# One low part per block moved from GpSimd to VectorE, and a new order of sums for the last 256 tokens, in an attention and feed-forward kernel

## The chip, the cores and the metric

The kernel runs on one core of a Trainium2 chip. The metric is the device time of one execution in microseconds (us). Before the change it is 1053.36 us, the median of three runs (1052.81 to 1054.94). One more execution was taken by the hardware profiler: it took 1052.79 us, of which the span from the first to the last instruction is 1050.6 us.

In this text PE is TensorE's matmul row, DVE is VectorE, ACT is ScalarE, POOL is GpSimd and SP is SyncE. SP, ACT and POOL can issue DMAs.

## What is computed

```python
# q, k, v: (8, 8, 576, 64); w_in: (512, 2048); w_out: (2048, 512); alpha: (2048,)
scores = q @ k.T / 8, masked to key blocks (of 64) up to the query's own
attn = softmax(scores)
x = (attn @ v) as (4608 tokens, 512)
h = x @ w_in
g = max(h, 0) + alpha * min(h, 0)
out = g @ w_out
```

All inputs and outputs are float32.

## The kernel before

The kernel has two stages. Until about 590 us it does the attention, and beside it the feed-forward products for 6 of the 16 blocks of 128 hidden features (FA = 6); their part of the output goes to a DRAM tensor `part`. From then on it does the other ten feature blocks in five pairs (NG = 5), and this is the stage that the change touches. Tokens go in nine blocks of 512 (`t0`, CHB), each in two halves of 256 (`h`, CHA).

A product of two float32 matrices is made of reduced-precision ones: each operand is split into a high part (a cast, on ACT) and a low part (source minus high part, on DVE or POOL; `split`, L422 to L426), and three matmuls are summed: high by high, and the two mixed ones. On top of that, a pair of feature blocks is multiplied in the seven-product (Strassen-Winograd) form, which trades the eighth product for sums of operands and of results. In the first layer (`pair1`, L612) each of the seven products has 6 matmuls of 256 columns into a PSUM bank; DVE and ACT combine the seven and apply the activation (L635, L639, L539, L541) into a tile `R` for each half. For the second layer `parts_of` (L668) makes the operands from `R`: `ha`, the high and low part of three quarters of `R`, and `hs`, the high and low part of four sums of quarters `S` (four additions of 128 columns on POOL, L441; a cast of 512 columns on ACT, L424; and the low part of 512 columns, L425, on POOL by `SLO`). `pair2` (L687) then runs 21 matmuls: the products 0, 1 and 6 read `ha`, the products 2 to 5 read `hs`. They add up over the five pairs (`i` = 0 to 4) in four banks: product n lies in bank n // 2, half n % 2. In each group of three matmuls the first two read the high part and the third reads the low part. After the fifth pair `finish` (L705) combines the seven sums on ACT and DVE (L718, L715), adds `part` (L441) and stores to `out`. Where `(h, i)` = (0, 4), then, is the last pair of the first half of a block.

In the last 256 tokens (the second half of the last block; the argument `end` or `tail`) other lists of engines hold (TSADD, TALO, TSLO), the four result tiles are stored by themselves, and the last pair runs in the order of products (0, 1), (2, 3), (4, 5), (6).

The order of instructions on each engine isn't written out: a planner (`Plan.schedule`, L141) simulates the engines with costs that stand in the code, and each engine then takes, of the operations that are ready in this simulation, the one with the lowest `prio`. PE's priorities follow the order of the calls. The result is a fixed sequence for each engine, and an engine that comes to an instruction whose input is late waits there, with all that is behind it. On the chip only true data dependencies make anyone wait. The costs in the code that matter here, in ns, are

```python
LAT = {"PE": 240, "DVE": 140, "ACT": 137, "POOL": 95}   # from an end to a reader on another engine
LONGER, TO_POOL, BESIDE = 1.06, 85, 480
c_dve(n) = 65 + n / 0.96; c_pool(n) = 145 + 2.1 * n     # times LONGER
# low part: POOL c_pool(n) + 60; DVE c_dve(n), and up to BESIDE more while POOL is busy
```

The next block's first-layer pairs are called early (TURNS, L50): the seven products of its first pair stand behind the second-layer products of (0, 4) in the priorities. PSUM has eight banks; four of them hold the sums of `pair2`.

Of the kernel before, what the change touches and what calls it, by code (L numbers as in the profile page):

```python
# [22 lines left out]
P = 128  # L23
# [27 lines left out]
XWHEN, UW, UX0 = 1, -30, -20  # L51
AGAIN, UA, UL = ((1, 4), (0, 4)), -20, -6
# [266 lines left out]
def attn_ffn(ctx, tc, qT, kT, vT, w_in, w_out, alpha, out):  # L319
# [348 lines left out]
    def parts_of(R, i, tail):  # L668
# [18 lines left out]
    def pair2(i, parts, accs, end):  # L687
# [4 lines left out]
        def run(todo):  # L692
            for n, b, x, w in todo:
                for k, (u, v) in enumerate(((0, 0), (0, 1), (1, 0))):
                    nc.tensor.matmul(accs[n // 2]()[:, CHA * (n % 2):CHA * (n % 2) + CHA], b()[:, u, P * x:P * x + P], W()[:, v, 256 * W2AT[w]:256 * W2AT[w] + 256],  # L695
                                     start=(first and k == 0 and n % 2 == 0), stop=(last and k == 2 and (n % 2 == 1 or n == 6)))
        ha, hs = parts
        last3 = ((0, ha, 0, "11"), (1, ha, 2, "21")), ((2, hs, 1, "t2"), (3, hs, 2, "t3")), ((4, hs, 0, "t1"), (5, hs, 3, "22")), ((6, ha, 1, "t4"),)
        for todo in last3 if end else ((*last3[0], *last3[3]), (*last3[1], *last3[2])):
            b = todo[0][1]  # L700
            fseq[0] += len(todo) / 2
            op("PE", 3 * len(todo) * c_mm(CHA), lambda todo=todo: run(todo), claim=[W],
               r=[(b, "h"), (b, "l"), *[((W, W2AT[w] // 2 * 2), x) for *_, w in todo for x in "hl"]], w=[accs[n] for n in sorted({n // 2 for n, *_ in todo})], prio=1.0e6 + fseq[0])

    def finish(accs, t0, end):  # L705
# [5 lines left out]
        def m(n):  # L711
            return lambda: accs[n // 2]()[:, CHA * (n % 2):CHA * (n % 2) + CHA]

        def plus(to, n, u):
            op("DVE", c_dve(CHA), lambda: nc.vector.tensor_tensor(out=to(), in0=m(n)(), in1=u(), op=ALU.add), r=[accs[n // 2], u], w=[to], prio=due(UM))  # L715
            return to
        u1 = Buf("u")
        op("ACT", c_act(CHA), lambda: nc.scalar.copy(out=u1(), in_=m(0)()), r=[accs[0]], w=[u1], prio=due(UM))  # L718
        u2 = plus(Buf("u"), 2, u1)
# [309 lines left out]
```

## Time and profile before

| what | value |
|---|---|
| median of three runs | 1053.36 us |
| profiled execution, whole time | 1052.79 us |
| its span | 1050.6 us |
| PE busy in the span | 981.7 us, 93% |
| POOL busy in the span | 774.2 us, 74% |
| DVE busy in the span | 865.7 us, 82% |
| granted TensorE clock, mean | 0.97 of full speed |

The page cuts the span in 40 slices of 26 us and gives each engine's busy share in tenths. A timeline row has the start (us), the length (us), the engine, the line, the operation, the tiles and the count of instructions merged; in brackets stands how long the engine was idle just before, and who ended that. Buffer numbers are left out of the tiles' names: `t` is any tile of 512 float32 columns, `u` one of 256, `X` the operands of the first layer (and of the second in the last 256 tokens).

### The profile page before, as it was taken

What the parts mean: (1) busy time and instruction counts of PE and PEld (TensorE: products, weight loads), DVE (VectorE), ACT (ScalarE), POOL (GpSimd) and SP (SyncE); (2) the same over time, 40 slices, a digit from 0 to 9 for tenths busy, and PEclk for the clock granted to TensorE, in tenths of its full rate; (3) what the DMA queues carried; (4) which work ended last, traced back from release to release, by engine and by line L of the source; (5) the groups of instructions that cost most, each with busy time, mean ns of one, the idle gap of its engine ahead of it and who ended that gap; (6) DMA issues with size and microseconds to landing.
All of it is one profiled execution on the core that took longest, in us unless ns stands there. A gap on an engine that the chain in (4) does not pass through costs nothing. (4 is left out here: it accounts for less than half of the span.)

```text
span 1050.6 us, 35000 instructions
## 1 busy us (share of the span) xinstructions
PE 981.7 (93%) x13670; PEld 900.5 (86%) x13670; DVE 865.7 (82%) x1923; ACT 626.6 (60%) x2158; POOL 774.2 (74%) x1320
## 2 busy tenths in 40 slices
PE   4578999999999999999999999999999999999997
PEld 3356778889888888888888989999999999999997
DVE  6999899988888877866586987888888888888877
ACT  7878787877777676756564554535353535444442
POOL 5887567656566665656499898888887979797964
PEclk7679999999999999999999999999999999999999
DMA  8455767576576566442372602030303031221211
GB/s 314 155 191 182 232 201 239 167 246 205 180 220 218 187 193 209 145 153 91 106 260 92 248 21 91 32 100 22 101 22 100 22 101 42 80 56 67 62 41 61
DMA packets 86485, 143.30 MB, mean 136 GB/s; under 512 B 12336, under 2 KB 50224, under 8 KB 86320
## 3 DMA queue, kind: packets, MB, share of 16 engines
q1 hardware_dynamic: 85744, 140.67, 41.1%
q8 instruction: 107, 1.75, 0.7%
q14 instruction: 58, 0.48, 0.1%
q10 hardware_dynamic: 576, 0.40, 0.1%
HBM read 103.82 MB, written 37.22 MB: 134 GB/s over the span
## 5 line engine op out<-in xcount | busy, mean ns | idle before, releaser
L844 ACT ACTIVATE p<-duo,c 128x256 f32<-128x256 f32 (+8 forms) x576 | 221.5, 415 | 40.9 <-DVE c L839 28.7
L626 PE MATMUL bank<-X,w 128*128 128x256 f32 x1890 | 239.1, 284 | 4.2 <-DVE t L541 3.0
L626 PEld LDWEIGHTS bank<-X,w 128*128 128x128 f32 x1890 | 231.5, 191 | 6.4 <-DVE t L541 4.2
L808 POOL TENSOR_SCALAR c<-c 32x4 f32<-32x4 f32 (+3 forms) x400 | 100.6, 252 | 87.4 <-DVE c L836 59.8
L441 POOL TENSOR_TENSOR t<-t 128x128 f32<-128x128 f32 (+1 forms) x180 | 102.5, 579 | 58.4 <-DVE t L541 38.6
L695 PE MATMUL bank<-w,hs 128*128 128x256 f32 x1020 | 137.3, 284 | 5.8 <-POOL hs L425 5.8
L568 PE MATMUL bank<-wa,gh 128*128 128x512 f32 x432 | 137.7, 400 | 4.3 <-POOL gh L550 2.3
L695 PEld LDWEIGHTS bank<-w,hs 128*128 128x128 f32 x1020 | 128.4, 190 | 7.7 <-POOL hs L425 7.4
L844 ACT ACTIVATION_READ_ACCUMULATOR p<-duo,c 128x1 f32 x576 | 130.2, 227 | 0.0
L529 PE MATMUL bank<-xh,wa 128*128 128x256 f32 x864 | 125.8, 287 | 1.5 <-DVE g L541 1.3
L441 POOL TENSOR_TENSOR t<-t,t 128x128 f32<-128x128 f32 (+1 forms) x200 | 123.2, 622 | 3.8 <-DVE w L425 1.3
L836 DVE TENSOR_REDUCE c<-duo 128x2 f32<-128x512 f32 (+8 forms) x288 | 121.4, 476 | 5.5 <-PE duo L831 5.3
L529 PEld LDWEIGHTS bank<-xh,wa 128*128 128x128 f32 x864 | 114.1, 192 | 10.4 <-issue 3.4
L425 POOL TENSOR_TENSOR hs<-t,hs 128x512 fp32r<-128x512 f32 x85 | 112.4, 1324 | 14.1 <-ACT hs L424 14.1
L424 ACT CAST hs<-t 128x512 fp32r<-128x512 f32 x85 | 52.7, 621 | 113.3 <-POOL t L441 111.1
L555 POOL TENSOR_TENSOR gl<-g,gh 128x256 fp32r<-128x256 f32 x108 | 84.5, 785 | 45.2 <-ACT gh L552 17.5
L848 DVE STREAM_TRANSPOSE PTH<-p 128x576 f32<-128x576 f32 (+4 forms) x160 | 99.8, 631 | 11.7 <-ACT p L844 10.4
L831 PE MATMUL duo<-k,q 64*32 64x288 f32 (+4 forms) x2560 | 86.5, 385 | 23.4 <-ACT p L844 18.3
L695 PE MATMUL bank<-w,ha 128*128 128x256 f32 x765 | 103.8, 282 | 0.0
L539 ACT ACTIVATE u<-bank 128x256 f32<-128x256 f32 x180 | 64.2, 382 | 59.8 <-DVE bank L639 58.4
L568 PEld LDWEIGHTS bank<-wa,gh 128*128 128x128 f32 x432 | 77.2, 188 | 23.6 <-issue 3.3
L695 PEld LDWEIGHTS bank<-w,ha 128*128 128x128 f32 x765 | 96.4, 189 | 0.2
(70 smaller groups left out, 1910.3 us busy)
## 6 DMA issues: line engine op xcount, KB each, us to landing
v<-in_v SPq DMA_DIRECT2D x32, 576.0 KB, 4.1
k<-in_k SPq DMA_DIRECT2D x32, 288.0 KB, 5.1
t<-xd SPq DMA_DIRECT2D x36, 256.0 KB, 4.2
t<-part SPq DMA_DIRECT2D x36, 256.0 KB, 2.7
out<-t SPq DMA_DIRECT2D x34, 256.0 KB, 2.1
va<-in_v SPq DMA_DIRECT2D x32, 256.0 KB, 3.3
raw<-in_w_in SPq DMA_DIRECT2D x16, 512.0 KB, 5.1
raw<-in_w_out SPq DMA_DIRECT2D x16, 512.0 KB, 4.4
```

Source lines behind the costliest of these rows:

```text
L425: op(on, c_pool(n) + 60 if on == "POOL" else Beside(c_dve(n)), lambda: (nc.gpsimd if on == "POOL" else nc.vector).tensor_tensor(out=lo(), ...
L441: op(e, c_pool(n) if e == "POOL" else Beside(c_dve(n)), lambda: (nc.gpsimd if e == "POOL" else nc.vector).tensor_tensor(out=to[1](), in0=a ...
L529: nc.tensor.matmul(hp()[:, :n], ww()[:, 0, cc * P:(cc + 1) * P], x()[:, cc, :n], start=(i == 0 and cc == 0), stop=(i == 2 and cc == NCC - 1))
L555: op("POOL", c_pool(CHA) + 60, lambda: nc.gpsimd.tensor_tensor(out=gl(), in0=g(), in1=gh().bitcast(F32), op=ALU.subtract), r=[g, gh], w=[g ...
L568: nc.tensor.matmul(acc(), a()[:, ts], ww(), start=(first and i == 0), stop=(last and i == 2))
L626: nc.tensor.matmul(bank()[:, :CHA], W()[:, i, 256 * at + P * c:256 * at + P * c + P], B()[:, j, CHA * c:CHA * c + CHA], start=(n == 0), st ...
L695: nc.tensor.matmul(accs[n // 2]()[:, CHA * (n % 2):CHA * (n % 2) + CHA], b()[:, u, P * x:P * x + P], W()[:, v, 256 * W2AT[w]:256 * W2AT[w] ...
L808: nc.gpsimd.tensor_scalar(out=o, in0=i, scalar1=scale, scalar2=None, op0=ALU.mult)
L831: nc.tensor.matmul(sb()[32 * i:32 * i + 32, h, off[T]:off[T] + w], q()[hs, qs], blocks(k()[hs], T + 1, 32 * (i % 2)), start=True, stop=True)
L836: op("DVE", c_dve(2 * w), lambda t=t, w=w, o=o: nc.vector.tensor_reduce(out=c()[:, 0, 2 * t:2 * t + 2], in_=sb()[:, :, o:o + w], axis=AX.X ...
L844: op("ACT", 237 + w / 1.2, lambda x=2 * t + h, T=T, h=h, w=w, o=o: nc.scalar.activation(out=pb()[:, 2 * o + h * w:2 * o + h * w + w], in_= ...
L848: op("DVE", 85 + 2.08 * w, lambda to=to, a=a, w=w, o=o: nc.vector.transpose(out=to()[:, a:a + 2 * w], in_=pb()[:, 2 * o:2 * o + 2 * w]), r ...
```

## The change

Three things are edited. First, in the blocks 0 to 3584 (eight of the nine) the low part of `hs` for (h, i) = (0, 4) is put on DVE instead of POOL (LAST_LOW). Second, for the last 256 tokens the products lie in the banks in another way (PLACE), the last pair runs in the order (0, 2), (6, 3), (4, 5), (1), and the earlier pairs are cut into one group more. Third, `finish` for these tokens adds the first partial sums to `part` on POOL, adds the rest onto the result tiles on DVE, stores in another order, and the loads of `part` depend, for the planner, on the block's last first-layer product. For all other tokens the functions are rewritten with the same operations in the same order.

```diff
+LAST_LOW = ((0, 4),)
...
-    def parts_of(R, i, tail):
+    def parts_of(R, i, tail, on=None):
...
-        split(lambda: Sb(), hi, lo, 512, [k for k, _ in s], (hs, "h"), (hs, "l"), (), slo[i % len(slo)], due(UP + 1.5))
+        split(lambda: Sb(), hi, lo, 512, [k for k, _ in s], (hs, "h"), (hs, "l"), (), on or slo[i % len(slo)], due(UP + 1.5))
...
+    PLACE = [{n: (n // 2, n % 2) for n in range(7)},
+             {0: (0, 0), 2: (0, 1), 3: (1, 0), 6: (1, 1), 4: (2, 0), 5: (2, 1), 1: (3, 0)}]
...
-        last3 = ((0, ha, 0, "11"), (1, ha, 2, "21")), ((2, hs, 1, "t2"), (3, hs, 2, "t3")), ((4, hs, 0, "t1"), (5, hs, 3, "22")), ((6, ha, 1, "t4"),)
-        for todo in last3 if end else ((*last3[0], *last3[3]), (*last3[1], *last3[2])):
+        opens, closes = (((0, 2, 4, 6), (1, 3, 5, 6)), ((0, 1, 4, 6), (1, 2, 3, 5)))[tail]
+        for ns in ((0, 1, 6), (2, 3, 4, 5)) if not tail else ((0, 2), (6, 3), (4, 5), (1,)) if last else ((0, 1), (6,), (2, 3, 4, 5)):
...
-            op("SP", 256, lambda b=b, t=t: nc.sync.dma_start(out=b(), in_=part[t:t + P, :]), r=[("part", t), ("part", t + 64), accs[0]], w=[(b, 0), (b, 1)], prio=0)
+            op("SP", 256, lambda b=b, t=t: nc.sync.dma_start(out=b(), in_=part[t:t + P, :]), r=[("part", t), ("part", t + 64), ("f1", t0 + CHA - CHB, NG - 1) if tail else accs[0]], w=[(b, 0), (b, 1)], prio=0)
...
+        u1 = new()
+        op("ACT", c_act(CHA), lambda: nc.scalar.copy(out=u1[1](), in_=part_of(accs, 0, tail)), r=[accs[0]], w=[u1[0]], prio=due(UM))
+        u2 = plus(new(), 2, u1)
+        if tail:
+            u3 = plus(new(), 3, u2)
+            add("POOL", CHA, c11, u1, c11, ALU.add, due(UM))
+            add("POOL", CHA, c12, u2, c12, ALU.add, due(UM))
+            add("POOL", CHA, c22, u3, c22, ALU.add, due(UM))
+            w21 = plus(new(), 6, u3)
+            plus(c12, 4, c12)
+            plus(c12, 5, c12)
+            plus(c22, 4, c22)
+            plus(c11, 1, c11)
+            add("POOL", CHA, c21, w21, c21, ALU.add, due(UM))
+            for k, (i, j, c) in enumerate(((0, 1, c12), (1, 0, c21), (1, 1, c22), (0, 0, c11))):
                 queue, issuer = (("SP", nc.sync), ("ACTQ", nc.scalar))[k % 2]
+                op(queue, 128, lambda c=c, t=t0 + P - P * i, j=j, issuer=issuer: issuer.dma_start(out=out[t:t + P, CHA * j:CHA * j + CHA], in_=c[1]()),
+                   r=[c[0]], prio=0)
+            return
...
-                    pair2(i, parts_of(Rs[t0, i][h], i, h and t0 + CHB == TOK), accs, h and t0 + CHB == TOK and i == NG - 1)
+                    pair2(i, parts_of(Rs[t0, i][h], i, tail, "DVE" if (h, i) in LAST_LOW and t0 + CHB < TOK else None), accs, tail)
```

Here `plus(to, n, u)` is one DVE addition of 256 columns, product n from its bank plus `u`, into `to`. Before, `finish` made with one ACT copy and seven such additions the four finished sums in `u` tiles, and then added them to the tiles loaded from `part`: the first two on POOL, the other two on DVE, each followed by its store.

## Rows read from the trace of the kernel before

**Rows 1.** The page: busy shares of PE and POOL in 40 slices of the span.

```profile
PE   4578999999999999999999999999999999999997
POOL 5887567656566665656499898888887979797964
```

**Rows 2.** Busy time of each engine in stretches; the columns are the stretch, its length, PE, PEld, DVE, ACT and POOL busy with instruction counts, granted clock, DMA share and GB/s. Two of the nine blocks, and the end.

```profile
729.40:780.40 51.00, 50.14 (x421) 49.93 (x421) 43.09 (x90) 23.27 (x54) 43.59 (x59) 1.00 0.21 63
...
831.20:882.00 50.80, 50.17 (x421) 49.96 (x421) 42.85 (x90) 23.31 (x54) 43.63 (x59) 1.00 0.21 64
...
1031.00:1050.60 19.60, 13.75 (x115) 13.54 (x114) 13.03 (x36) 3.07 (x6) 5.94 (x5) 0.96 0.24 81
```

**Rows 3.** The waits of PE from 560 us on: waiter, what it waited for, us in total, times, longest.

```profile
PE bank L695 <- POOL hs L425: 5.8, 8, 0.9
PE bank L626 <- DVE t L541: 3.0, 3, 1.5
PE bank L626 <- DVE u L635: 0.6, 1, 0.6
```

**Rows 4.** PE's timeline around (0, 4) of the block at 2048; the 36 matmuls of L626 are six products of the next block.

```profile
825.77 4.48 PE L626 MATMUL bank<-X,w 128*128 128x256 f32 x36
830.09 0.40 PE L695 MATMUL bank<-w,hs 128*128 128x256 f32 x2
831.11 1.45 PE L695 MATMUL bank<-w,hs 128*128 128x256 f32 x10 [0.63 <-POOL hs L425]
```

**Rows 5.** PE's timeline at the same place in the second and the fourth block, and at (0, 4) of the last block: the first, the third and the last of eight such waits (rows 4 has the fourth).

```profile
676.47 0.40 PE L695 MATMUL bank<-w,hs 128*128 128x256 f32 x2
677.54 1.45 PE L695 MATMUL bank<-w,hs 128*128 128x256 f32 x10 [0.67 <-POOL hs L425]
...
779.06 0.40 PE L695 MATMUL bank<-w,hs 128*128 128x256 f32 x2
780.32 1.45 PE L695 MATMUL bank<-w,hs 128*128 128x256 f32 x10 [0.86 <-POOL hs L425]
...
1030.72 1.45 PE L695 MATMUL bank<-w,hs 128*128 128x256 f32 x10 [0.84 <-POOL hs L425]
```

**Rows 6.** The timeline of POOL and ACT around the same place as rows 4: the fourth addition of `S`, three additions for the next half, ACT's cast, and the low part.

```profile
828.11 0.46 POOL L441 TENSOR_TENSOR t<-t,t 128x128 f32<-128x128 f32 x1
828.52 0.88 POOL L441 TENSOR_TENSOR t<-t 128x128 f32<-128x128 f32 x2
828.60 0.62 ACT L424 CAST hs<-t 128x512 fp32r<-128x512 f32 x1 [1.54 <-POOL t L441]
829.12 0.38 ACT L539 ACTIVATE u<-bank 128x256 f32<-128x256 f32 x1
829.37 0.46 POOL L441 TENSOR_TENSOR t<-t,t 128x128 f32<-128x128 f32 x1
829.79 1.27 POOL L425 TENSOR_TENSOR hs<-t,hs 128x512 fp32r<-128x512 f32 x1
```

**Rows 7.** DVE's timeline: low parts of 512 columns for `X`, and then what DVE does around rows 4.

```profile
816.93 0.84 DVE L425 TENSOR_TENSOR X<-t,X 128x512 fp32r<-128x512 f32 x1
820.58 1.12 DVE L425 TENSOR_TENSOR X<-t,X 128x512 fp32r<-128x512 f32 x1
824.47 1.78 DVE L425 TENSOR_TENSOR X<-t,X 128x512 fp32r<-128x512 f32 x1
...
828.12 0.43 DVE L639 TENSOR_TENSOR bank<-bank,u 128x256 f32<-128x256 f32 x1 [0.23 <-PE bank L626]
828.85 0.42 DVE L635 TENSOR_TENSOR u<-bank,u 128x256 f32<-128x256 f32 x1 [0.29 <-PE bank L626]
829.54 0.48 DVE L541 SCALAR_TENSOR_TENSOR t<-u,oal,bank 128x256 f32<-128x256 f32 x1 [0.27 <-ACT u L539]
```

**Rows 8.** DVE's low parts of `X` over the whole trace: count, shortest, median and longest in ns.

```profile
L425 DVE TENSOR_TENSOR X<-t,X x32: 675/1096/1782, 527.8 to 1039.1; 128x512 fp32r<-128x512 f32 x32
```

**Rows 9.** The first block's (0, 4): the timeline of 624 to 628 us, and the stretch from 626 to 628 us (columns as in rows 2).

```profile
624.74 0.62 ACT L424 CAST hs<-t 128x512 fp32r<-128x512 f32 x1
625.38 1.43 PE L626 MATMUL bank<-X,w 128*128 128x256 f32 x6 [1.36 <-DVE t L541]
626.61 2.69 PE L695 MATMUL bank<-w,hs 128*128 128x256 f32 x12
...
626.00:628.00 2.00, 2.00 (x11) 2.00 (x11) 1.41 (x4) 0.75 (x3) 2.00 (x4) 0.50 0.00 0
```

**Rows 10.** The end of the kernel, engine by engine (timeline).

```profile
1040.75 4.00 PE L695 MATMUL bank<-w,X 128*128 128x256 f32 x32
1042.99 0.38 ACT L718 COPY u<-bank 128x256 f32<-128x256 f32 x1 [3.96 <-PE bank L695]
1043.78 2.67 DVE L715 TENSOR_TENSOR u<-bank,u 128x256 f32<-128x256 f32 x7 [3.03 <-PE bank L695]
1044.74 0.72 POOL L441 TENSOR_TENSOR t<-t,u 128x256 f32<-128x256 f32 x1 [4.88 <-DVE u L715]
1046.36 0.84 DVE L441 TENSOR_TENSOR t<-t,u 128x256 f32<-128x256 f32 x2
1047.24 0.86 ACTq L731 DMA_DIRECT2D out<-t  x2
```

More of the change, by code (lines that the diff above doesn't have):

```diff
@@ L714, in plus @@
         def plus(to, n, u):
[L715 removed]
+            op("DVE", c_dve(CHA), lambda: nc.vector.tensor_tensor(out=to[1](), in0=part_of(accs, n, tail), in1=u[1](), op=ALU.add), r=[accs[PLACE[tail][n][0]], u[0]], w=[to[0]], prio=due(UM))
             return to
[L717 to L718 removed]
@@ L719, in finish @@
-        u2 = plus(Buf("u"), 2, u1)
-        c11 = plus(u1, 1, u1)
-        u3 = plus(Buf("u"), 3, u2)
-        u4 = plus(Buf("u"), 4, u2)
-        c22 = plus(u2, 4, u3)
-        c12 = plus(u4, 5, u4)
-        c21 = plus(u3, 6, u3)
-        for k, (c, i, j) in enumerate(((c11, 0, 0), (c22, 1, 1), (c12, 0, 1), (c21, 1, 0))):
-            add(("POOL", "POOL", "DVE", "DVE")[k] if end else OADD, CHA, ((o[i], j), lambda i=i, j=j: o[i]()[:, CHA * j:CHA * j + CHA]), ((o[i], j), lambda i=i, j=j: o[i]()[:, CHA * j:CHA * j + CHA]),
-                (c, lambda c=c: c()), ALU.add, due(UO))
-            if end:
-                queue, issuer = (("SP", nc.sync), ("ACTQ", nc.scalar))[k % 2]
-                op(queue, 128, lambda b=o[i], t=t0 + P - P * i, j=j, issuer=issuer: issuer.dma_start(out=out[t:t + P, CHA * j:CHA * j + CHA], in_=b()[:, CHA * j:CHA * j + CHA]),
-                   r=[(o[i], j)], prio=0)
@@ L733, in finish, with new @@
-        for b, t in () if end else zip(o, (t0 + P, t0)):
+        def new():
+            u = Buf("u")
+            return u, lambda: u()
+        c11, c12, c21, c22 = (sides(i, j) for i in range(2) for j in range(2))
+        u1 = new()
[13 more added lines that the diff above has]
+            for k, (i, j, c) in enumerate(((0, 1, c12), (1, 0, c21), (1, 1, c22), (0, 0, c11))):
+                queue, issuer = (("SP", nc.sync), ("ACTQ", nc.scalar))[k % 2]
+                op(queue, 128, lambda c=c, t=t0 + P - P * i, j=j, issuer=issuer: issuer.dma_start(out=out[t:t + P, CHA * j:CHA * j + CHA], in_=c[1]()),
+                   r=[c[0]], prio=0)
+            return
@@ L734, in finish @@
+        w11 = plus(u1, 1, u1)
+        u3 = plus(new(), 3, u2)
+        u4 = plus(new(), 4, u2)
+        w22 = plus(u2, 4, u3)
+        w12 = plus(u4, 5, u4)
+        w21 = plus(u3, 6, u3)
+        for c, u in ((c11, w11), (c22, w22), (c12, w12), (c21, w21)):
+            add(OADD, CHA, c, c, u, ALU.add, due(UO))
+        for b, t in zip(o, (t0 + P, t0)):
             op("SP", 256, lambda b=b, t=t: nc.sync.dma_start(out=out[t:t + P, :], in_=b()), r=[(b, 0), (b, 1)], prio=0)
```

25 lines of the change are left out of this document (16 added, 9 removed).

## The prediction

> **What bounds the kernel now.** I read the slices of the page first, to see where the changed code runs. From about the 23rd slice PE is at nine tenths or more in every slice and POOL at seven to nine [rows 1]. Busy time by block then shows how tight that is: in a block of 50.8 to 51.0 us PE is busy 50.14 to 50.17, so under 1 us of a block is idle, while DVE has 8 and POOL 7 us to spare [rows 2]. PE sets the time of this stage, and taking load from POOL pays only where PE waits for POOL. The list of PE's waits says where: of the 9.4 us in its three largest rows, 5.8 are eight waits for the low part of `hs` on POOL [rows 3]. The timeline puts them all at one place. The group `hs` of (0, 4) starts, runs the two matmuls that read the high part and stands until the low part is there [rows 4, 5]. Matmuls follow each other at (830.09 - 825.77) / 36 = 0.12 us [rows 4], so the third was due at 830.09 + 0.24 = 830.33 and came at 831.11: 0.78 us lost. The same sum gives 0.83 and 1.02 for the second and fourth block [rows 5]. The eighth wait is the last block's, which LAST_LOW leaves out. So seven waits of 0.8 to 1.0 us, together about 6, are what the first edit can win.
>
> **The low part on DVE: its length.** On POOL the cast ends at 828.60 + 0.62 = 829.22, an addition stands ahead, and the low part runs from 829.79 for 1.27 us to 831.06; PE starts 0.05 later [rows 6, 4]. No row shows this operation on DVE, but the same one on `X` (512 columns, both inputs in SBUF) took 0.68 us at the shortest, 1.10 in the median and 1.78 at the longest [rows 8]. Which of these holds depends on POOL's work beside it: 0.84 at 816.93, and 1.12 and 1.78 further on [rows 7]. Beside (0, 4) POOL has additions of 0.46 us [rows 6], so I take 0.84 and keep 0.68 and 1.12 as bounds. DVE passes from ACT fast (the activation on ACT ends at 829.12 + 0.38 = 829.50, DVE starts at 829.54 [rows 6, 7]). Taking the same 0.05 as above on both sides, the low part runs from 829.27 to 830.11 and PE may go on at 830.16, with bounds of 830.00 and 830.44. That is 0.95 us before the 831.11 of now. POOL is spared 1.27 us, which is worth nothing in itself.
>
> **The order.** If PE came to `hs` when it does now, the third matmul would be due at 830.33 and the wait would be gone. But the sequence is remade by the planner, which starts the group when its own figures say that the low part is ready. They are figures for an order, and I take no time of the chip from them. From the cast's end they give, with POOL, (137 + 85) + 1.06 x 1280 + 95 = 1.67 us, and more when an addition stands ahead, as it does in the trace; with DVE 137 + 1.06 x 598 + 140 = 0.91, up to 1.39 when POOL is busy beside it. So the planner believes in 0.3 to 0.8 us less, up to 0.4 more than that for the addition. A product of the next block is 6 x 0.12 = 0.72 us, and products aren't split. Now the group stands behind the sixth product, so by the planner's figures the low part came between the fifth and the sixth. With some 0.6 us less it most likely goes behind the fifth: PE reaches it at 829.37, the third matmul is due at 829.61, the low part is there at 830.16, and 0.55 us is lost instead of 0.78 (bounds 0.39 and 0.83). That gains 0.23 us a block, 7 x 0.23 = 1.6 us in all (bounds -0.3 and +2.7). The planner was over 1 us too early before and is so after; the move takes away the low part's length and hands most of it to an earlier start.
>
> **What the low part holds up.** DVE runs in order. By the planner's figures the low part stands ahead of the L639 of 828.12 and the L635 of 828.85 [rows 7], so these wait behind it until 830.1, nearly 2 us. Behind them is the release of first-layer banks: the seventh product of the next block needs the third one's bank, which then comes free after L639 (0.43), ACT's activation (0.38) and L541 (0.48), at about 831.4 [rows 6, 7]. PE wants it after the ten other `hs` matmuls (830.16 + 1.2) and the sixth product (0.72), at 832.1. I cost it at nothing, with 0.7 us of cover; without it, each 0.1 us more costs 0.7 us over seven blocks.
>
> **The first block** is not like the others. Its low part isn't waited for; PE waits 1.36 us for the activation on DVE and then runs `hs` in 2.69 us, at a granted clock of 0.50 (the lower of the two levels, 1.2 GHz) between 626 and 628 us [rows 9], where the twelve take 12 x 0.12 = 1.4 at the upper one. A low part of 0.84 us right after the cast of 624.74 comes before that activation on DVE, so the wait can grow by up to 0.8; or `hs` goes ahead and fills it, which can save as much, and the 1.3 us of slow clock with it. I take 0, bounds -2 and +1.
>
> **The last 256 tokens.** PE's last matmul ends at 1044.75 [rows 10]. The last stores are two issues on ACT from 1047.24, 0.43 us each, so the last goes out at 1047.67; the one DMA that decides is the last. Before, the first sum was read at 1042.99 and DVE waited for bank 1 until 1043.78, then had seven additions in 2.67 us (0.38 each) and two more, until 1047.20 [rows 10]. After, products 0 and 2 share the first bank, so u2 starts when ACT's copy is done, 1042.99 + 0.38 + 0.05 = 1043.42, and u3 and w21 follow to 1044.6 at 0.4 each. POOL adds c11, c12, c22 from 1043.42 at 0.72 each [rows 10]: 1044.14, 1044.86, 1045.58. DVE's `c12 += 4` waits for POOL's second until 1044.9, and behind it in DVE's order are the last three; with 0.4 each they end at 1045.3, 1045.7, 1046.1 and 1046.5. c21 ends on POOL at 1046.4. The last two issues on ACT then start at 1046.45 and 1046.88: 0.8 us before 1047.67. If POOL is held up by DVE, or the stores go out closer together than now and their transfers queue, less: bounds 0 and 1.1. The reordering within PE costs nothing as long as the last `hs` is ready 0.7 us earlier, and the loads of `part` move to an earlier place in SP's queue, where only stores stand; the trace shows POOL waiting for DVE, not for a load [rows 10].
>
> The sum: 1.6 + 0 + 0.8 = 2.4 us. From the profiled execution's 1052.79 that is 1050.4; the median of the runs is 0.57 higher (1053.36), and on that the forecast is 1050.9 us, with a range of its own of 1048.5 to 1053.0.
>
> A rule speaks against the first edit. The rows show the same low part on DVE at anything from 0.68 to 1.78 us, with POOL at work beside it [rows 7, 8]. The Trainium skill (SBUF — State Buffer, "Who interferes with whom") says that a VectorE instruction with two SBUF inputs contends with a GpSimd instruction that reads SBUF, and that the one that comes later is blocked until the other ends. The spread of the rows agrees with it, though no row here separates the wait from the work; what it would make of the sum is the third rival.
>
> **The rivals.**
> 1. The order stays, or the planner's gain doesn't reach the fifth product. Then all of the waits go: seven times 0.78 to 1.02 is 6.0 us, with the end 6.8: 1046.6 us. For it: the low part is there at 830.16, before 830.33. Against it: the planner needs only some 0.4 us less, on average, to move the group. Chance 0.2.
> 2. The group moves by two products (slower than before). PE then reaches it at 828.65 and the third matmul is due at 828.89, while the low part still comes at 830.16: 1.27 us lost instead of 0.78, 0.49 x 7 = 3.4 us, less 0.8 at the end: 1053.36 + 2.6 = 1056.0. It decides from 0.72 us of the planner's gain on, if the low part was thought ready just after the fifth product. For it: the gain of 0.3 to 0.8 plus 0.4 can reach that. Against it: its figure for DVE beside a busy POOL takes back up to 0.48. Chance 0.15.
> 3. DVE's low part is held up by POOL, or DVE by it: 0.68 + an addition of 0.46 = 1.14 us ends at 830.41, PE goes on at 830.46, and a group one product earlier loses 0.85, as much as now. Only the end is left: 1052.6 us. For it: low parts of 1.12 and 1.78 [rows 7]. Against it: those stand beside POOL work of other kinds. Chance 0.2.
>
> **How the numbers follow.** The forecast has 0.45, the rivals 0.2, 0.15 and 0.2. The range runs from the first rival's side to short of the second's, and leaves out about 2 in 10: 1046.8 to 1055.4. What a measurement can tell from no change is about 0.2%, 2.1 us. Faster by that: 0.45 x 0.65 (the forecast lies just beyond it) + 0.2 + a little of the third = 0.52. Slower: 0.15 x 0.8, and 0.04 for the first block or a new wait behind the low part = 0.16. The rest, 0.32, is within 0.2%.
>
> **What would show it.** Right: in PE's waits the seven become waits for DVE's `hs` of some 0.4 us, five products (30 matmuls) of L626 between `ha` and `hs` of (0, 4), DVE low parts of about 0.84 us, and last issues near 1046.9. Wrong: 36 matmuls still and no wait (rival 1), 24 and longer waits (rival 2), low parts over 1.1 us (rival 3), or new waits of L626 for DVE's L639 and L541.

## The result, and the profile after

| | before | after |
|---|---|---|
| median of 15 runs each | 1053.31 us | 1060.62 us |
| lowest and highest | 1050.93 to 1054.94 | 1052.84 to 1074.67 |
| profiled execution, its span | 1052.79, 1050.6 | 1055.35, 1053.6 |

The changed kernel is slower: ratio 1.0064, 95% interval 1.0044 to 1.0083. (Ratios leave out single runs more than 1.5% above the fastest of a kernel, so for a kernel that scatters this much they lie below the ratio of the medians.) The scatter is itself a finding: 22 us between two runs of one program, where before had 4. (Before isn't always so even: of 28 later runs of it, beside the first experiments, one took 1061.82 us, the others 1049.67 to 1056.43.)

The lines have moved by the edit: the low part is L426 (was L425), the cast L425, the additions of `S` L442, the matmuls L627 and L704, DVE's combining L636, L640 and L542.

The list of PE's waits from 560 us on (waiter, what it waited for, us in total, times, longest) answers to [rows 3]:

```profile
PE bank L627 <- DVE t L542: 4.5, 5, 2.3
PE bank L704 <- POOL hs L426: 4.0, 8, 0.9
PE bank L704 <- DVE hs L426: 1.8, 8, 0.2
PE bank L627 <- DVE u L636: 1.3, 2, 0.7
```

The 5.8 us of waits for POOL's `hs` have become 1.8 for DVE's `hs` and 4.0 for POOL's: the same sum, in two places of a block (the last block's wait of 0.85 us is in it as before). And one wait of 2.3 us for L542 is new. PE's timeline shows the two places in the block at 1024 (719.81 to 732.11) and the block with the long wait (878.75 to 934.23); the two rows ahead of these are from the first block, and the last is the end:

```profile
617.78 1.23 PE L704 MATMUL bank<-w,ha 128*128 128x256 f32 x9
...
624.95 2.31 PE L627 MATMUL bank<-X,w 128*128 128x256 f32 x18
...
719.81 3.75 PE L627 MATMUL bank<-X,w 128*128 128x256 f32 x30
723.46 0.50 PE L704 MATMUL bank<-w,hs 128*128 128x256 f32 x2
724.20 1.44 PE L704 MATMUL bank<-w,hs 128*128 128x256 f32 x10 [0.23 <-DVE hs L426]
...
729.74 1.80 PE L704 MATMUL bank<-w,hs 128*128 128x256 f32 x14
732.11 1.44 PE L704 MATMUL bank<-w,hs 128*128 128x256 f32 x10 [0.56 <-POOL hs L426]
...
775.61 1.45 PE L704 MATMUL bank<-w,hs 128*128 128x256 f32 x10 [0.23 <-DVE hs L426]
...
878.75 1.46 PE L704 MATMUL bank<-w,hs 128*128 128x256 f32 x10 [0.24 <-DVE hs L426]
...
892.27 4.18 PE L627 MATMUL bank<-X,w 128*128 128x256 f32 x18 [2.34 <-DVE t L542]
...
934.23 1.45 PE L704 MATMUL bank<-w,hs 128*128 128x256 f32 x10 [0.23 <-DVE hs L426]
...
1035.83 12.74 PE L704 MATMUL bank<-w,X 128*128 128x256 f32 x105
```

(0, 4) is as forecast: 30 matmuls of the next block ahead of `hs` instead of 36, and the third matmul, due at 723.46 + 0.24 = 723.70, comes at 724.20, 0.50 us late. New is a wait in the group of (1, 1), the second pair of the next half: its fifteenth matmul is due at 729.74 + 14 x 0.12 = 731.42 and comes at 732.11, 0.69 late; before, these 24 ran in one piece. Together 1.19 us a block are lost where 0.78 were. Of the 0.69, 0.33 comes from POOL's low part, which takes 1.62 us there instead of 1.29 (its row is below); in the next block it takes 1.32, and PE comes 0.36 late. From one (0, 4) to the next it is 775.61 - 724.20 = 51.41 us; before it was 831.11 - 780.32 = 50.79 [rows 4, 5]. The early blocks of before are longer, so that the six from its second (0, 4) to its eighth take 983.52 - 677.54 = 305.98, 51.00 each. Once the changed kernel has 934.23 - 878.75 = 55.48.

POOL and DVE show what happened in that block. DVE first: the low part that was moved, and a low part of `ha`, which belongs to (1, 2), in three blocks.

```profile
723.44 0.70 DVE L426 TENSOR_TENSOR hs<-t,hs 128x512 fp32r<-128x512 f32 x1 [1.51 <-ACT hs L425]
...
730.33 0.58 DVE L426 TENSOR_TENSOR ha<-t,ha 128x384 fp32r<-128x384 f32 x1
...
781.74 1.82 DVE L426 TENSOR_TENSOR ha<-t,ha 128x384 fp32r<-128x384 f32 x1
...
884.88 6.95 DVE L426 TENSOR_TENSOR ha<-t,ha 128x384 fp32r<-128x384 f32 x1
```

One instruction, the low part of `ha`, takes 0.58, 1.82 or 6.95 us. Over the whole trace the low parts of `ha` on DVE are (count, shortest, median and longest in ns)

```profile
L426 DVE TENSOR_TENSOR ha<-t,ha x51: 542/811/6951, 593.2 to 1030.3; 128x384 fp32r<-128x384 f32 x51
```

so the longest is more than eight times the median. POOL's timeline at the first and the last of these:

```profile
727.91 0.47 POOL L442 TENSOR_TENSOR t<-t,t 128x128 f32<-128x128 f32 x1
728.33 0.47 POOL L442 TENSOR_TENSOR t<-t 128x128 f32<-128x128 f32 x1
728.75 0.90 POOL L442 TENSOR_TENSOR t<-t,t 128x128 f32<-128x128 f32 x2
729.59 0.47 POOL L442 TENSOR_TENSOR t<-t 128x128 f32<-128x128 f32 x1
730.01 0.48 POOL L442 TENSOR_TENSOR t<-t,t 128x128 f32<-128x128 f32 x1
730.44 1.62 POOL L426 TENSOR_TENSOR hs<-t,hs 128x512 fp32r<-128x512 f32 x1
...
885.00 1.29 POOL L426 TENSOR_TENSOR hs<-t,hs 128x512 fp32r<-128x512 f32 x1
886.24 0.88 POOL L442 TENSOR_TENSOR t<-t 128x128 f32<-128x128 f32 x2
887.07 0.46 POOL L442 TENSOR_TENSOR t<-t,t 128x128 f32<-128x128 f32 x1
887.49 1.02 POOL L426 TENSOR_TENSOR ha<-t,ha 128x384 fp32r<-128x384 f32 x1
888.47 1.29 POOL L426 TENSOR_TENSOR hs<-t,hs 128x512 fp32r<-128x512 f32 x1
889.73 0.45 POOL L442 TENSOR_TENSOR t<-t,t 128x128 f32<-128x128 f32 x1
890.14 0.86 POOL L442 TENSOR_TENSOR t<-t 128x128 f32<-128x128 f32 x2
890.96 0.45 POOL L442 TENSOR_TENSOR t<-t,t 128x128 f32<-128x128 f32 x1
895.30 1.30 POOL L426 TENSOR_TENSOR hs<-t,hs 128x512 fp32r<-128x512 f32 x1 [3.89 <-ACT hs L425]
```

In the first, DVE's 0.58 runs through and POOL's `hs` takes 1.62 instead of 1.29. In the last, POOL works without a gap through ten instructions, until it runs dry at 890.96 + 0.45 = 891.41, and DVE's instruction ends at 884.88 + 6.95 = 891.83, 0.42 later. The 1.82 of 781.74 ends in the same way 0.41 behind one POOL instruction, a low part of 1.32 us from 781.83. During the 6.95 ACT and PE wait for DVE, and POOL at last for ACT; PE idles 2.34 us, and then its clock drops. The stretches that follow (columns as in [rows 2]):

```profile
892.00:894.00 2.00, 1.63 (x7) 1.34 (x7) 2.00 (x7) 0.00 (x0) 0.00 (x0) 0.59 0.00 0
894.00:896.00 2.00, 2.00 (x10) 2.00 (x11) 1.81 (x6) 0.95 (x3) 0.70 (x1) 0.55 0.94 282
```

At a granted clock of 0.55 to 0.59, near the lower level (1.2 GHz), the 18 matmuls of 892.27 take 4.18 us instead of 2.31. The block's 55.48 us are 4.1 more than the usual 51.4: that is what one such instruction, a hold from here on, costs.

Two parts went well. The first block no longer has its stretch at clock 0.50 [rows 9], as the stretch below from 622.5 to 625.5 us shows (clock 1.00): PE goes from the start of the `ha` before (0, 4) to the three products after it in 624.95 - 617.78 = 7.17 us, before in 629.14 - 619.46 = 9.68. At the end, PE's last matmul ends at 1035.83 + 12.74 = 1048.57, 5.03 us before the span's end; before it was 1050.6 - 1044.75 = 5.85.

That stretch of the changed kernel, and PE's timeline of before:

```profile
622.50:625.50 3.00, 2.35 (x17) 2.15 (x18) 2.60 (x7) 2.24 (x6) 3.00 (x4) 1.00 0.00 0
...
619.46 1.23 PE L695 MATMUL bank<-w,ha 128*128 128x256 f32 x9
...
629.14 2.30 PE L626 MATMUL bank<-X,w 128*128 128x256 f32 x18
```

### The profile page after: what moved, and what is told of

Its sections match the earlier page's. It is cut to its first block, busy times and chain, and to the rows that moved or that the text cites. A ratio compares the mean times of both kernels' runs of the same rounds, so it can differ in the third digit from the quotient of the medians.

```text
span 1053.6 us, 34991 instructions
## 1 busy us (share of the span) xinstructions
PE 983.0 (93%) x13670; PEld 899.4 (85%) x13670; DVE 874.4 (83%) x1929; ACT 629.5 (60%) x2158; POOL 770.0 (73%) x1314
## 3 DMA queue, kind: packets, MB, share of 16 engines
q8 instruction: 107, 1.75, 0.7%
## 4 chain that ended last, share of the span: by engine, by line
PE 63%; POOL 14%; DVE 12%; issue 5%; ACT 4%; DMA 2%; DVEq 0%; POOLq 0%; ACTq 0%; SPq 0%
PE bank L627 16%; PE bank L704 16%; PE bank L530 10%; PE bank L569 10%; PE duo L859 6%; PE duo L918 6%; POOL t L442 5%; ACT p L872 2%; POOL gl L556 2%; DVE c L864 2%; POOL c L836 1%; DVE t L542 1%; POOL hs L426 1%; DVE u L727 1%; DVE ha L426 1%
## 5 line engine op out<-in xcount | busy, mean ns | idle before, releaser
L627 PE MATMUL bank<-X,w 128*128 128x256 f32 x1890 | 238.8, 283 | 6.5 <-DVE t L542 4.5
L627 PEld LDWEIGHTS bank<-X,w 128*128 128x128 f32 x1890 | 230.7, 191 | 9.3 <-DVE t L542 5.8
L442 POOL TENSOR_TENSOR t<-t 128x128 f32<-128x128 f32 (+1 forms) x180 | 104.8, 593 | 71.0 <-DVE t L542 63.2
L704 PE MATMUL bank<-w,hs 128*128 128x256 f32 x1020 | 138.8, 284 | 6.5 <-POOL hs L426 4.0
L704 PEld LDWEIGHTS bank<-w,hs 128*128 128x128 f32 x1020 | 127.5, 189 | 11.0 <-POOL hs L426 5.7
L442 POOL TENSOR_TENSOR t<-t,t 128x128 f32<-128x128 f32 (+1 forms) x200 | 121.9, 614 | 4.4 <-DVE w L426 1.2
L426 POOL TENSOR_TENSOR hs<-t,hs 128x512 fp32r<-128x512 f32 x77 | 103.2, 1341 | 13.1 <-ACT hs L425 13.1
L704 PE MATMUL bank<-w,ha 128*128 128x256 f32 x765 | 103.7, 282 | 0.4 <-DVE ha L426 0.4
L425 ACT CAST hs<-t 128x512 fp32r<-128x512 f32 x85 | 52.8, 621 | 77.5 <-POOL t L442 65.9
L704 PEld LDWEIGHTS bank<-w,ha 128*128 128x128 f32 x765 | 96.3, 189 | 0.6 <-DVE ha L426 0.6
```

The lines of the kernel that those rows point to most:

```text
L426: op(on, c_pool(n) + 60 if on == "POOL" else Beside(c_dve(n)), lambda: (nc.gpsimd if on == "POOL" else nc.vector).tensor_tensor(out=lo(), ...
L442: op(e, c_pool(n) if e == "POOL" else Beside(c_dve(n)), lambda: (nc.gpsimd if e == "POOL" else nc.vector).tensor_tensor(out=to[1](), in0=a ...
L627: nc.tensor.matmul(bank()[:, :CHA], W()[:, i, 256 * at + P * c:256 * at + P * c + P], B()[:, j, CHA * c:CHA * c + CHA], start=(n == 0), st ...
L704: nc.tensor.matmul(part_of(accs, n, tail), b()[:, u, P * x:P * x + P], W()[:, v, 256 * W2AT[w]:256 * W2AT[w] + 256], start=(first and k == ...
```

## The experiments

The expectations name three theories. P (port): DVE's instructions with two SBUF inputs are held by POOL's, far longer than one POOL instruction, and the holds make the loss. O (order): the planner's new sequence has more steady waits than the old one, hold or no hold. T (tail): the new end costs time, by itself or by what it displaces. A hold is a DVE instruction of over 5 us, counted in the one profiled run of each kernel. Ratios are to before, measured at the same time; its medians were 1051.5 to 1052.7 us there. In the code, "..." marks what is left out.

**Which edit.** The first edit alone, on the kernel before:

```diff
+LAST_LOW = ((0, 4),)
...
-        split(lambda: Sb(), hi, lo, 512, [k for k, _ in s], (hs, "h"), (hs, "l"), (), slo[i % len(slo)], due(UP + 1.5))
+        split(lambda: Sb(), hi, lo, 512, [k for k, _ in s], (hs, "h"), (hs, "l"), (), on or slo[i % len(slo)], due(UP + 1.5))
...
```

> The kernel before with the first edit alone (LAST_LOW); the end is as before. Theory P (port): the loss comes from the first edit, because GpSimd's instructions now follow each other without a gap where VectorE has the low part of ha for (1, 2), and VectorE's instruction, with two inputs in SBUF, is held until GpSimd rests; that costs about 4 us whenever it happens and not in each block, so the runs scatter. Expected 1056 to 1066 us, median near 1061, a spread of more than 5 us. Theory O (order): the loss is regular, the new wait for hs of (1, 1), 0.6 us in each of seven blocks: 1057 to 1058 us with a spread under 3 us. Theory T (the end): the loss comes from the new end or from its loads: then this kernel is at 1050 to 1052 us.

1060.25 us (1050.36 to 1067.64), ratio 1.0041 (1.0007 to 1.0074), two holds in the profiled run (their blocks take 55.35 and 56.14 us, 4.0 and 4.7 above 51.4): loss and scatter are there without the new end, and O alone doesn't explain such a scatter. The second edit alone is the changed kernel with

```diff
-LAST_LOW = ((0, 4),)
+LAST_LOW = ()
```

> The changed kernel without the first edit (LAST_LOW empty): only the last 256 tokens are new. Theories P and O: 0.8 us less than before, 1052.5 us, with the spread of before (under 4 us). Theory T: 1058 us or more.

1050.37 us (1049.44 to 1051.29), ratio 0.9976 (0.9958 to 0.9993). T falls: the end gains 1.9 us in the medians (0.7 to 4.4 by the interval).

**Engine or order.** The first edit moves an operation to another engine and has the sequence remade. The next two kernels part these: `split` gets an argument `run` for the engine that issues, while `on` is the one that the planner sees. Order kept, planned as POOL's and issued on DVE:

```diff
...
-        op(on, c_pool(n) + 60 if on == "POOL" else Beside(c_dve(n)), lambda: (nc.gpsimd if on == "POOL" else nc.vector).tensor_tensor(
+        op(on, c_pool(n) + 60 if on == "POOL" else Beside(c_dve(n)), lambda: (nc.gpsimd if (run or on) == "POOL" else nc.vector).tensor_tensor(
...
-        split(lambda: Sb(), hi, lo, 512, [k for k, _ in s], (hs, "h"), (hs, "l"), (), on or slo[i % len(slo)], due(UP + 1.5))
+        split(lambda: Sb(), hi, lo, 512, [k for k, _ in s], (hs, "h"), (hs, "l"), (), slo[i % len(slo)], due(UP + 1.5), on)
```

> The changed kernel, but the planner still takes the low part of (0, 4) for an operation of GpSimd with GpSimd's cost, so the order of all engines stays that of before, and only the issue goes to VectorE. The wait of 0.78 to 1.02 us goes away in seven blocks, and 0.8 us at the end. Theory O: that is all, 1046.6 to 1048 us, small spread. Theory P: GpSimd is still 1.27 us ahead in each block from there on; if its run without a gap then covers VectorE's low part of (1, 2), instructions of more than 2 us show on VectorE and the runs scatter above 1050 us; if not, 1046.6 to 1048 us as well, with no such instruction in the trace.

1046.32 us (1044.33 to 1049.08), ratio 0.9942 (0.9922 to 0.9963): faster than both kernels, with no hold and little scatter, and the two theories' common figure (1046.6 to 1048). PE's timeline of it:

```profile
829.35 1.60 PE L704 MATMUL bank<-w,hs 128*128 128x256 f32 x12
...
875.17 4.48 PE L627 MATMUL bank<-X,w 128*128 128x256 f32 x36
879.49 1.60 PE L704 MATMUL bank<-w,hs 128*128 128x256 f32 x12
...
885.19 2.98 PE L704 MATMUL bank<-w,hs 128*128 128x256 f32 x24
```

36 matmuls again ahead of `hs`, and both groups in one piece. From 829.35 to 879.49 it is 50.14 us, 1.27 less than in the changed kernel, near the 1.19 lost there; the six blocks from the second (0, 4) to the eighth take 979.71 - 677.33 = 302.38. The timelines of POOL and DVE show why (1, 1) doesn't wait, and what the low part of `ha` for (1, 2) does in this order:

```profile
883.86 0.47 POOL L442 TENSOR_TENSOR t<-t,t 128x128 f32<-128x128 f32 x1
884.29 0.89 POOL L442 TENSOR_TENSOR t<-t 128x128 f32<-128x128 f32 x2
885.13 1.31 POOL L426 TENSOR_TENSOR hs<-t,hs 128x512 fp32r<-128x512 f32 x1
885.69 1.17 DVE L426 TENSOR_TENSOR ha<-t,ha 128x384 fp32r<-128x384 f32 x1
```

Between two low parts POOL has three additions, and this low part starts with PE's group; in the changed kernel six stand ahead of it (727.91 to 730.44 above), and it starts 0.70 after the group. DVE's low part starts 0.56 behind POOL's here and ends 0.42 behind its end, at 886.86: it too is held, but for one POOL instruction only, 1.17 us instead of 0.58. Before, whose order this is, shows the same: in the third to eighth block of both kernels this instruction takes 1.14 to 1.35 us. In the new order it starts about 0.1 us ahead of POOL's low part, and takes 0.58, 1.82 or 6.95.

Order only, planned as DVE's and issued on POOL:

```diff
+        split(lambda: Sb(), hi, lo, 512, [k for k, _ in s], (hs, "h"), (hs, "l"), (), on or slo[i % len(slo)], due(UP + 1.5), "POOL" if on else None)
```

> The changed kernel with the planner's order of the change (it takes the low part for VectorE's), but the low part is issued on GpSimd. PE comes to hs one product (0.72 us) earlier than before and the low part comes as late as before, so 0.78 + 0.72 = 1.5 us are lost per block there. Both theories: 7 x 0.72 more than before, less 0.8 at the end, 1057.6 us. Theory P: without the scatter, since GpSimd isn't ahead (spread under 4 us, no VectorE low part over 2 us). Theory O: with the second wait for hs of (1, 1) on top, 1061 us or more.

1084.8 us (1079.39 to 1091.84), ratio 1.0301 (1.0259 to 1.0344), far above the 1057.6 that both theories start from. The waits at (0, 4) of 1.3 us were expected; the holds were not: 6 of 8 blocks have one of 6.93 to 6.96 us, though POOL has the 1.27 us of the low part again. In the old order there is no hold, whether DVE (the kernel above) or POOL (before) has that low part. So the holds come with the new sequence, not from POOL having less to do.

The order-kept kernel for all nine blocks:

```diff
-                    pair2(i, parts_of(Rs[t0, i][h], i, tail, "DVE" if (h, i) in LAST_LOW and t0 + CHB < TOK else None), accs, tail)
+                    pair2(i, parts_of(Rs[t0, i][h], i, tail, "DVE" if (h, i) in LAST_LOW else None), accs, tail)
```

> The version with the order of before and the low part of (0, 4) issued on VectorE, now in all nine blocks. The last block's wait of 0.85 us goes as well: 0.8 us less than with eight blocks, 1045.5 us, without scatter and without a VectorE instruction over 2 us. If the last block's low part comes in the way of something else there: 1046 to 1047 us.

1047.0 us (1043.56 to 1050.51), ratio 0.9944 (0.9924 to 0.9964): the same as the eight blocks, within what can be told, and not the 0.8 us less that was expected.

**What a hold needs.** Three kernels shift the moment or the engine of one instruction of the changed kernel. `first` is issued in front of a low part, by another argument of `split`; of each line only this argument is shown. A memset of one column on DVE in front of the low part of `ha` for (1, 2):

```diff
...
+first=(lambda: nc.vector.memset(idle, 0.0)) if (h, i) == (1, 2) and not tail else None
...
```

> The changed kernel with one more instruction on VectorE: a memset of one column of a tile that nobody reads, right before the low part of ha for (1, 2) in each block. It puts this low part some 0.1 us later, so that it no longer comes 0.12 us before GpSimd's low part of hs for (1, 1) but with it or behind it. Theory P (whoever reaches the shared port second is held, and VectorE is held over GpSimd's whole run): held in nearly every block, about 7 us long, some 4 us lost each time: 1080 to 1086 us, little scatter. Rival R (the loss is in the order alone and the long instruction a symptom of something it waits for by data): 1060 us, as the change.

1060.42 us (1056.88 to 1062.36), two holds. That is rival R's time, but the memset ran beside the instruction after it, which started 0.09 to 0.12 us ahead of POOL's as in the changed kernel. Nothing was moved, so this one tells nothing for or against either.

The same on POOL, in front of the low part of `hs` for (1, 1):

```diff
...
+first=(lambda: nc.gpsimd.memset(idle, 0.0)) if (h, i) == (1, 1) and not tail else None
...
```

> The changed kernel with one more instruction on GpSimd: a memset of one column of a tile that nobody reads, right before the low part of hs for (1, 1) in each block, some 0.1 us or more. VectorE's low part of ha for (1, 2) then comes first to the port in every block. Theory P: no VectorE instruction over 2 us, 1050 to 1052.5 us, spread under 4 us, though GpSimd does more than in the change. Rival R: 1060 us and more, as the change.

1053.33 us (1050.33 to 1055.97), ratio 1.001 (0.9998 to 1.0022): no hold, and a little over the 1050 to 1052.5 of theory P. DVE's low part takes 0.57 to 0.58 us in all seven later blocks, where it now starts 0.14 to 0.16 us ahead of POOL's (whose low part then takes 1.56 to 1.58), while PE's two waits a block stay. The second and the eighth (0, 4) on PE:

```profile
676.51 1.45 PE L705 MATMUL bank<-w,hs 128*128 128x256 f32 x10 [0.24 <-DVE hs L427]
...
984.66 1.45 PE L705 MATMUL bank<-w,hs 128*128 128x256 f32 x10 [0.22 <-DVE hs L427]
```

The six blocks take 308.15 us, where before took 305.98 and the order kept 302.38. In the medians the holds cost 1060.6 - 1053.3 = 7.3 us, and the steady part of the new order 1053.3 - 1046.3 = 7.0. These medians were not taken side by side: before had 1053.3 beside the first, 1052.2 beside the second and 1052.3 beside the third, so the 7.3 is good to about 1 us.

The low part of `ha` for (1, 2) issued on POOL:

```diff
...
+run="POOL" if (h, i) == (1, 2) and not tail else None
...
```

> The changed kernel in its own order, but the low part of ha for (1, 2) is issued on GpSimd, so the instruction that was held isn't on VectorE. Theory P: no VectorE instruction over 2 us and a spread under 4 us; GpSimd has 1.0 us more ahead of the low part of hs for (1, 1), which PE waits for already (0.7 us a block), so between 1051 and 1058 us. Rival R: the scatter of the change stays (over 5 us).

1068.68 us (1060.33 to 1069.19), ratio 1.0138 (1.0108 to 1.0168): a miss. With the low part of `ha` gone from DVE, the next DVE instructions with two SBUF inputs, the additions to `part`, are held instead; in three blocks one of the four takes 6.9 us:

```profile
733.83 7.91 DVE L442 TENSOR_TENSOR t<-t,u 128x256 f32<-128x256 f32 x4
```

Two more memsets on POOL stand in the order-only kernel with its six holds. In the middle of POOL's run:

```diff
...
+first=(lambda: nc.gpsimd.memset(idle, 0.0)) if (h, i) == (1, 3) and not tail else None
...
```

> The kernel of e4 (the order of the change, the low part of (0, 4) issued on GpSimd; six long holds in its trace, 1084.8 us) with one GpSimd memset of one column of an unused tile right before the low part of ha for (1, 3), in the middle of GpSimd's run, 2.5 us behind the place where VectorE is held. Theory P: VectorE gets the port there; its low part of ha for (1, 2) takes about 2.9 us instead of 6.95 where it is held, and most of the 4 us per hold come back: 1060 to 1072 us. Rival (VectorE waits for data or for something in another queue, and GpSimd's run ends because of the same): still 6.95 us and 1080 us or more.

1086.34 us (1081.06 to 1090.27), seven holds of 6.97 to 7.00, as the rival said. But the memset overlapped its neighbours and left no gap, so whether a gap in the run sets DVE free wasn't tried by it.

And ahead of the run, with `(h, i) == (1, 1)` in front of the low part of `hs`, as above:

> The kernel of e4 with the same memset right before the low part of hs for (1, 1), ahead of the place where VectorE is held. Theory P: no hold, VectorE's low part 0.6 us in each block, and what is left is the order's own loss: 1055 to 1061 us. Rival: 1080 us or more, as e4.

1068.17 us (1059.15 to 1069.05), between the two figures, with two holds instead of six: ahead of the run it helps, as in the changed kernel, but not always. One of the two differs from all other holds here, as DVE came free without POOL running dry. It also started 0.27 us behind POOL's low part, where the other low parts with a hold start 0.08 to 0.14 ahead. DVE's row, and POOL's instruction at the end of it:

```profile
631.90 6.57 DVE L427 TENSOR_TENSOR ha<-t,ha 128x384 fp32r<-128x384 f32 x1 [0.74 <-ACT ha L426]
...
638.01 1.59 POOL L427 TENSOR_TENSOR hs<-t,hs 128x512 fp32r<-128x512 f32 x1
```

POOL's instruction before it ends at 638.06, the hold 0.41 later, at 638.47; POOL goes on without a gap, and it is POOL's next low part that takes 1.59.

**One input.** In the order-only kernel the low part of `ha` for (1, 2) is replaced by a reduction over a dimension of one element, which has one SBUF input. It copies the source, so the low part isn't computed there.

```diff
...
+(lambda: nc.vector.tensor_reduce(out=lo(), in_=src().unsqueeze(2), axis=AX.X, op=ALU.max)) if alone else
...
```

> The kernel of e4, whose low part of ha for (1, 2) was held for 7 us in six blocks. Here this low part is replaced by a reduction over a dimension of one element, which copies the source and has one input in SBUF instead of two (so the low part isn't computed there: it holds the value itself). Theory P (the hold is at the port that the second SBUF input uses): the replaced instruction is never held, about 0.5 us in each block; the four additions to part behind it, which have two inputs in SBUF, may be held in its place in some blocks; 1055 to 1075 us. Rival (VectorE waits there for something else): the replaced instruction still takes 7 us in most blocks, 1080 us or more.

1078.18 us (1074.15 to 1082.48), a little over theory P's 1055 to 1075. The replaced instruction takes 0.54 to 0.55 us in all eight blocks; in seven of them the hold goes to the next one that reads two SBUF inputs, the first of the four additions, which alone takes 5.91 to 5.94 (DVE's timeline):

```profile
682.44 0.54 DVE L426 TENSOR_REDUCE ha<-t 128x384 fp32r<-128x384 f32 x1
682.98 0.48 DVE L542 SCALAR_TENSOR_TENSOR t<-u,oal,bank 128x256 f32<-128x256 f32 x1
683.38 6.93 DVE L442 TENSOR_TENSOR t<-t,u 128x256 f32<-128x256 f32 x4
```

L542, whose second tensor lies in PSUM, passes in between. And POOL again runs without a gap until 689.03 and then starves for ACT:

```profile
688.56 0.47 POOL L442 TENSOR_TENSOR t<-t,t 128x128 f32<-128x128 f32 x1
692.04 1.28 POOL L426 TENSOR_TENSOR hs<-t,hs 128x512 fp32r<-128x512 f32 x1 [3.02 <-ACT hs L425]
```

**The hold by itself.** Three tests stand behind the whole kernel before, so their total times mean nothing. DVE waits out a chain of memsets of varied length and then does one instruction of 384 columns, while POOL does a dozen or so in a row:

```diff
...
+            for _ in range(12):
+                nc.gpsimd.tensor_tensor(out=pa[:, :P], in0=ra[:, :P], in1=rb[:, :P], op=ALU.add)
...
+            nc.vector.tensor_tensor(out=va[:, :3 * P], in0=ra[:, :3 * P], in1=second[:, :3 * P], op=ALU.add)
```

> The kernel before, and behind its last instruction a test that computes nothing of the output: 26 times GpSimd runs 12 additions of 128 columns in a row, and VectorE issues one addition of 384 columns on other tiles somewhere in this run, at 13 phases 40 columns of memset apart; 13 times with both inputs in SBUF, 13 times with the second one in PSUM. No data pass between the two in the run. Theory P: with both inputs in SBUF VectorE's addition takes either about 0.55 us or most of what is left of the run (2 to 4 us), with one in PSUM always about 0.5 us. Rival R: never more than one GpSimd addition longer (1.0 us), with either.

0.56 to 0.82 us with both inputs in SBUF, rising and falling with the phase, and always 0.55 with the second in PSUM. Held, but only for the rest of one POOL instruction, and not the 2 to 4 us of theory P. The next lets POOL's instructions write to different places, as in the kernel, with a low part of 512 among them:

> The test of the shared port behind the kernel before once more, but GpSimd's additions now write different places, so that each starts before the last one has ended, as the kernel's do (0.42 us from start to start, 0.46 long). Three sets of 16 phases, 32 columns of memset apart: VectorE's two inputs in SBUF beside additions alone; the same with a subtraction of 512 columns as GpSimd's fourth instruction; and that with VectorE's second input in PSUM. Theory P: in the first two sets some phases are held over the rest of GpSimd's run (over 2 us) and the others take 0.55 us or end with GpSimd's next instruction; in the third set all take 0.55. Rival: a hold never lasts longer than the GpSimd instruction at work (1.8 us at most), as the first test showed; then the 7 us of the changed kernel need another cause.

0.56 to 1.68 us, and 0.55 to 0.56 with PSUM. The last takes the kernel's own widths and phases about a nanosecond apart:

> The test of the port a third time: GpSimd runs the changed kernel's own sequence of widths (128, 128, 128, 512, 128, 128, 128, 384, 512, 128 four times), VectorE one subtraction of 384 columns on other tiles. 50 phases lie one column of memset (about 1 ns) apart around the start of the 512, where the second test's outcome turned from 0.56 to 1.68 us; 63 more lie 5 columns apart within the 512. Theory P, narrowed (a hold over the whole run needs both to reach the port at nearly the same moment): a few of the 50 phases, or a few ends of the 512, take more than 4 us, the others 0.56 or up to 1.8. Rival: all take 0.56 to 1.8 us; then a hold over several instructions needs something of the kernel that this test lacks, and stays unexplained.

0.56, or 1.35 to 1.69, flipping between 0.56 and 1.69 within 1 to 2 ns of phase; no long hold in 113 phases. All three came out as the rival said. So it is shown that a DVE instruction with two SBUF inputs can be held by POOL's work, and that it is these instructions that the kernel's holds strike. What makes a hold last beyond one POOL instruction in the kernel is not in these tests, and stays open.

## Why the prediction was wrong

It said 1050.9 us and faster; 1060.6 and slower was measured.

**The bound and the place: right.** PE's waits at (0, 4) were the thing to win. Rival 1, with its order kept, would give 1046.6; the kernel that keeps the order has 1046.32. That they agree so closely is luck: the move gave 4.1 us there, not 6.0, the end 1.9, not 0.8, and before was 1.0 lower beside it. (The slices of the page were read loosely: PE is at nine tenths from the fifth slice on, and the last slice is lower; nothing hangs on it.)

**The order: right.** One product earlier, 30 matmuls; 0.55 us lost forecast, 0.50 measured. The low part on DVE was put at 0.84 (0.68 to 1.12) and takes 0.70 (0.69 to 0.71 in the eight blocks).

**"What the low part holds up … I cost it at nothing": the step that failed.** It followed the low part on DVE as far as the seventh product's bank, and there the cover held. What the remade order does further on was put at nothing without a reason, and both losses come from there. The first is a steady one: in (1, 1) POOL has six additions ahead of a low part, three in the order kept, and PE loses 0.36 to 0.69 us more. The forecast's gain of 0.23 us a block, 1.6 in all, became a loss: six blocks take 308.15 us without holds and 305.98 before, 0.36 a block and, by that, an estimated 2.5 over seven (between the later blocks shown it is 51.41 - 50.79 = 0.62). The second, and the larger, are the holds.

**Rival 3 had the cause of the holds, and was mis-sized.** It priced a hold of DVE by POOL at one addition, 0.46 us, and looked for it at `hs`. It struck `ha` of (1, 2) for up to 6.95 us, at 4.1 us each with the slow clock after it. By that price the 7.3 us between the medians with and without holds would be about 1.8 of them a run, an estimate; the two profiled runs with the first edit have one and two. [Rows 7] had shown 0.84, 1.12 and 1.78 for one operation; I read that as a spread of the low part moved, and not as a risk for every DVE instruction that the new order sets beside POOL's run.

The Trainium skill (SBUF — State Buffer, "Who interferes with whom") says which VectorE instructions can be held: those with two SBUF inputs, beside a GpSimd instruction that reads SBUF, while with at most one SBUF input they don't contend outside the 2-port modes; the reduction's 0.54 us in eight blocks, the 0.55 with PSUM and the additions held in its stead agree. The Trainium skill (SBUF — State Buffer, "SBUF: two separate sides") also says that the one who starts first has the ports for the whole instruction and the other is blocked. By that a hold ends with one GpSimd instruction, as in the three tests (at most 1.69 us) and in the order kept (1.17); the kernel's 6.95 over ten of them is more than that, and there the trace has DVE starting 0.12 us ahead.

**The first block** was put at 0 (-2 to +1) and gained 9.68 - 7.17 = 2.5 us, beyond the bound: `hs` went ahead, filled the wait, and the slow clock went with it, the good case that the text named. **The end** was put at 0.8 and shows 5.85 - 5.03 = 0.8 in the profiled runs, 1.9 in the medians. DVE's last addition was to end 1.75 us after PE's last matmul; it ends 1.65 after it (at 1050.22), before 2.45.

**The sum** with these terms, an estimate: 2.5 for the new order, -2.5 for the first block, -0.8 for the end and 7.3 for the holds are 6.5 us more than before; 1060.6 - 1053.3 = 7.3 was measured.

Step by step in the medians: 1052.3 before, 1050.4 with the new end, 1046.3 with the low part on DVE in the old order (4.1 less), 1053.3 in the new order without holds (7.0 more), 1060.6 with them (7.3 more). The profiled runs bear out the 7.0 roughly: their spans differ by 1052.6 - 1045.9 = 6.7 us, their six blocks by 308.15 - 302.38 = 5.8. The first edit is thus two: the move, worth 4.1 us, and the new order that the planner made for it, which took 14.3 back. That the memset in the kernel without holds does nothing else to its time was not tried by itself.

## What to carry to other kernels

When a planner or a scheduler remakes a sequence, an edit's own cost can be the smaller part (here 4.1 us gained, 14.3 lost by the new order): follow the new order a whole period on, at every engine, or issue the changed instruction in the old order and compare. In a profile, look for an instruction whose longest time is many times its median (here 6951 against 811 ns for `ha`): such a row was the sign of the holds, in a kernel whose runs scatter. A VectorE instruction with two SBUF inputs next to a long gapless run of GpSimd work is a risk; one with its second input in PSUM, or with one input, was never held here.

## What the runs showed of the hardware

- The text ahead of the prediction says that on the chip only data dependencies make anyone wait. The tests behind the kernel show another wait: no data pass between the two engines in GpSimd's run, and VectorE's instruction takes up to 1.69 us instead of 0.56.
- In the kernel a VectorE instruction with two SBUF inputs was held through a whole run of ten GpSimd instructions, 6.95 us, and ended 0.42 us after that run stopped. All holds but one ended like this (0.28 to 0.42 us after); that one ended while GpSimd went on. In the order of before it is held for one GpSimd instruction (1.17 us), and in the tests for one at most.
- VectorE instructions that read one tensor in PSUM and one in SBUF took 0.40 to 0.48 us, all 7911 of them from 590 us on in before, the changed kernel and the eleven variants of them above, beside the same GpSimd work.
- Whether such an instruction is held can't be told from the start times in a trace. In the changed kernel's later blocks the low part of `ha` starts 0.11 to 0.13 us ahead of GpSimd's low part where it wins (0.58 us, and GpSimd then takes 1.6 instead of 1.3), and 0.09 and 0.12 ahead where it loses (1.82 and 6.95); in the test the outcome flipped within 1 to 2 ns. The scatter goes with it: 1052.8 to 1074.7 us in the changed kernel, 1050.3 to 1056.0 in the one whose profiled run has no hold.
- One memset of one column on GpSimd, 0.10 us, in front of the run: the changed kernel's profiled run then has no hold and its median is 7.3 us lower, while the order-only kernel goes from six holds to two. In the middle of the run it left that kernel with seven.
